# FFT mixing and a three-way maxout network on one core: how the first batch's rows are fetched, cast and reversed

## Chip, core and metric

One core of one Trainium2 chip runs the whole program. The metric is the device time of one execution in microseconds (us). The core has five engines with queues of their own: TensorE (PE, matmuls; its weight loads are listed as PEld), VectorE (DVE), ScalarE (ACT), GpSimd (POOL) and SyncE (SP). DMA transfers are issued here by SP, ACT and POOL, and are carried out by 16 DMA engines that all queues share. Each engine works through its own instructions in order; engines wait for each other through semaphores.

## What is computed

```python
def _attn_ref(x):                       # x: 8 x 3072 x 256, fp32
    X = np.fft.fft(x, axis=1)
    X = np.fft.fft(X, axis=2)
    return X.real.astype(np.float32)

def _moe_ref(x, w1, w2, w3, w_out):     # 24576 tokens, 256 -> 768 -> 256
    h = np.maximum(np.maximum(x @ w1, x @ w2), x @ w3)
    return (h @ w_out).astype(np.float32)
```

The output is `_moe_ref` of the tokens that `_attn_ref` gives.

## The kernel before

A batch of x is 3072 rows of 256 features. The row number is split as 128 a + bb (a below 24, bb below 128), the feature number as 64 g + dl (g below 4). A batch lies in SBUF on 96 partitions (g, a), and each partition holds 128 pieces ("rows" bb) of 64 features dl. The Fourier transform over the row number is done in two steps, first over a (24 values, `Mix.s`), then over bb (128 values, `Mix.k`); the transform over the features is folded into the network's weights (`prep_first`, `prep_second`). Because x is real, the kernel works on x and on x with its rows in reverse order: `Mix.s` multiplies, for each dl, the forward rows (line 415) and the reversed rows of the mirrored feature 64 - dl (line 417), and accumulates both. For batches 1 to 7 POOL makes the bf16 copies of x, forward and reversed, while PE works on the batch before (`turn_chunk`).

Batch 0 has nothing to hide behind, and is handled apart, in the straight code that the change touches:

- Rows 0 to 79 are loaded by POOL (lines 178, 186, 190), which casts them to bf16 on the way, straight into the forward tile `x0_first` (`x0`, `x0v`). `load_rows` issues four transfers, one for each g, of 24 partitions each.
- Rows 80 to 127 are loaded as fp32 into the staging tiles `xs` by SP and ACT (lines 163 to 170), and row 128, which is row 0 of the next a, by `load_next`: four transfers of 23 partitions and one of 4. Here rows 80 to 95 go by SP, 96 to 111 by ACT, then by SP row 128 and after it rows 112 to 127.
- The reversed rows lie in `back` (`xr0`), one line of 130 rows for each dl from 32 to 64. `reverse(copy, xr, xs, r0, n, d0, d1)` writes the reversed copy of rows r0 to r0 + n - 1 for dl from d0 to d1 - 1; the engine is the one whose `copy` it is given.
- The staged rows are cast into `x0_first` by DVE (line 331) and reversed for dl 32 to 63 by ACT (line 332). Then ACT makes `md_all`, the sines of the feature angles (line 333), and the rest is reversed from `x0_first` by ACT and DVE (lines 334 to 339).
- The feature angles `vm` (lines 309 to 326) are made on DVE, ahead of the casts. `nmd_all` is `md_all` negated (line 340), `tab_minus` negates a part of the sine table of the second step (lines 307, 341).
- While rows arrive, PE runs 17 matmuls on the sine table whose result is not used (`warm`, lines 608 to 610). Then come the groups s0 to s6 of batch 0 (line 614; s0 uses dl 2 to 6, and so reversed dl 58 to 62; s1 uses dl 7 to 11), the first folded weights (line 617) and the steps of the second transform.
- SP, after the transfers of batch 0, loads batch 1 (line 348), each of these transfers behind the landing of the weights' first half. POOL, after the rows, issues the weights (lines 193 to 201).

The order on each engine is the order of the program's text; nothing is rescheduled.

Of the kernel before, what the change touches and what calls it, by code (L numbers as in the profile page):

```python
# [9 lines left out]
FP32 = mybir.dt.float32  # L10
BF16 = mybir.dt.bfloat16
# [22 lines left out]
def kernel(  # L34
# [9 lines left out]
    nc = tc.nc  # L44
# [48 lines left out]
    def x_rows(b):  # L93
        return x[b].rearrange("(a bb) (g dl) -> g a bb dl", bb=128, g=4)

    def load_rows(eng, dst, b, r0, r1, after=None):
        xr = x_rows(b)
        for g in range(4):
            ld = eng.dma_start(out=dst[g * 24:(g + 1) * 24], in_=xr[g, :, r0:r1, :])  # L99
            if after is not None:  # L100
                tc.add_manual_dep(ld.ins, after.ins.name, AFTER, reason="weights first")

    def load_next(eng, dst, b, after=None):

        xr = x_rows(b)
        parts = [(dst[g * 24: g * 24 + 23], xr[g, 1:24, 0:1, :]) for g in range(4)]
        parts.append((dst[23:96:24], xr[:, 0, 0:1, :]))
        for (to, src) in parts:
            ld = eng.dma_start(out=to, in_=src)
            if after is not None:  # L110
                tc.add_manual_dep(ld.ins, after.ins.name, AFTER, reason="weights first")
# [13 lines left out]
    def reverse(copy, xr, xs, r0, n, d0=32, d1=65):  # L125

        last = r0 + n > 128
        for (lo, hi, m) in ((d0, min(d1, 64), n), (64, d1, n - 1)) if last else ((d0, d1, n),):
            if lo < hi:
                copy(out=xr[:, lo - 32:hi - 32, 129 - r0 - m:129 - r0],  # L130
                     in_=bass.AP(xs.tensor, xs.offset + (m - 1) * 64 + lo,
                                 [xs.ap[0], [1, hi - lo], [-64, m]]))
# [19 lines left out]
    gen = gen_pool_cm.__enter__()  # L152
# [3 lines left out]
    def iota(t, pattern, base=0, cm=0):  # L156
        nc.gpsimd.iota(t, pattern, base=base, channel_multiplier=cm,
                       allow_small_or_imprecise_dtypes=True)

    x0_first = x0_pool.tile([96, 64 * 130], BF16, name="x0", tag="x0")  # L160
    x0v = x0_first.rearrange("p (bb dl) -> p bb dl", dl=64)
    staged = []
    for (r0, eng) in ((80, nc.sync), (96, nc.scalar), (112, nc.sync)):
        n = 17 if r0 == 112 else 16
        xs = xs_pool.tile([96, 33 * 64], FP32, name="xs", tag="xs")
        xv = xs[:, 0:n * 64].rearrange("p (bb dl) -> p bb dl", dl=64)
        if n > 16:
            load_next(eng, xv[:, 16:17, :], 0)
        load_rows(eng, xv[:, 0:16, :], 0, r0, r0 + 16)
        staged.append((r0, n, xs))  # L170

    pidx = gen.tile([128, 1], FP32, tag="pidx")
    iota(pidx, [[0, 1]], cm=1)
# [1 line left out]
    iota(j128, [[1, 128]])  # L175
    i13 = gen.tile([128, 13], FP32, tag="i13")
    iota(i13, [[1, 13]])
    load_rows(nc.gpsimd, x0v[:, 0:32, :], 0, 0, 32)
    jm24 = gen.tile([96, 48], FP32, tag="jm24")
    iota(jm24[:, 0:13], [[1, 13]])  # L180
    iota(jm24[:, 13:24], [[-1, 11]], base=-1)
# [1 line left out]
    iota(jm24[:, 37:48], [[1, 11]], base=1)  # L183
    g24 = gen.tile([96, 5], FP32, tag="g24")
    iota(g24, [[24, 5]])
    load_rows(nc.gpsimd, x0v[:, 32:64, :], 0, 32, 64)
    dvec = gen.tile([128, 128], FP32, tag="dvec")
    iota(dvec.rearrange("p (dl g) -> p dl g", g=4), [[1, 32], [64, 4]])
    iota(dvec[:, 2:4], [[64, 2]], base=32)
    load_rows(nc.gpsimd, x0v[:, 64:80, :], 0, 64, 80)  # L190

    first_half = None
    for jh in range(2):
        for wsrc, wdst in ((moe_w1, w1_bf), (moe_w2, w2_bf), (moe_w3, w3_bf)):
            wld = nc.gpsimd.dma_start(
                out=wdst.rearrange("p (fc j) -> p fc j", fc=2)[:, :, jh * 384:(jh + 1) * 384],
                in_=wsrc.rearrange("(fc p) j -> p fc j", fc=2)[:, :, jh * 384:(jh + 1) * 384])
        if jh == 0:
            first_half = wld
    nc.gpsimd.dma_start(out=wout_bf.rearrange("p (jc c) -> p jc c", jc=NJC),  # L200
                        in_=moe_w_out.rearrange("(jc p) c -> p jc c", jc=NJC))
# [16 lines left out]
    nc.vector.memset(z[:, :, 24:26], 0.0)  # L218
    nc.vector.memset(m0f[:, 50:52], 0.0)
    nc.vector.memset(m0r[:, 50:52], 0.0)  # L220
    half = gen.tile([128, 256], FP32, tag="half")
    nc.vector.memset(half[:, 0:128], 64.0)
    nc.vector.memset(half[:, 128:256], 0.0)

    p128 = gen.tile([128, 1], FP32, tag="p128")
    nc.vector.tensor_scalar(out=p128, in0=pidx, scalar1=1.0 / 128.0, scalar2=None, op0=ALU.mult)
# [30 lines left out]
    def tab_minus(r0, r1):  # L257
        nc.vector.tensor_scalar(out=tabs[:, r0:r1, 2, :], in0=tabs[:, r0:r1, 0, :],
                                scalar1=-1.0, scalar2=None, op0=ALU.mult)
# [36 lines left out]
    for (m, c, by) in ((m24f, 0, ind24), (m24r, 24, ind24[:, ::-1])):  # L296
        nc.vector.tensor_tensor(
            out=m.rearrange("p (g r) -> p g r", g=4),
# [7 lines left out]

    tab_minus(0, 7)

    vm = gen.tile([128, 512], FP32, tag="vm")
    qm = gen.tile([128, 512], FP32, tag="qm")  # L310
    pf = gen.tile([128, 2], FP32, tag="pf")
    half = gen.tile([128, 256], FP32, tag="half")
    nc.vector.memset(half[:, 0:128], 64.0)
    nc.vector.memset(half[:, 128:256], 0.0)
    for fc in range(2):
# [3 lines left out]
            out=vm[:, fc * 256:(fc + 1) * 256].rearrange("p (k c) -> p k c", c=128),  # L319
# [5 lines left out]
    nc.vector.scalar_tensor_tensor(out=vm, in0=qm, scalar=-256.0 * ROUND, in1=vm,  # L325
                                   op0=ALU.add, op1=ALU.subtract)

    back = gen.tile([96, 33 * 130], BF16, tag="back")
    xr0 = back.rearrange("p (dl bb) -> p dl bb", bb=130)
    for (r0, n, xs) in staged:  # L330
        nc.vector.tensor_copy(out=x0_first[:, r0 * 64:(r0 + n) * 64], in_=xs[:, 0:n * 64])
        reverse(nc.scalar.copy, xr0, xs, r0, n, 32, 64)
    nc.scalar.activation(out=md_all, in_=vm, func=AX.Sin, scale=float(-2.0 * math.pi / 256.0))
    for (copy, r0, n, d0, d1) in ((nc.scalar.copy, 80, 49, 64, 65),
                                  (nc.scalar.copy, 0, 31, 32, 65),
                                  (nc.vector.tensor_copy, 31, 32, 32, 65),
                                  (nc.scalar.copy, 63, 17, 32, 49),
                                  (nc.vector.tensor_copy, 63, 17, 49, 65)):
        reverse(copy, xr0, x0_first[:, r0 * 64:(r0 + n) * 64], r0, n, d0, d1)
    nc.vector.tensor_scalar(out=nmd_all, in0=md_all, scalar1=-1.0, scalar2=None, op0=ALU.mult)  # L340
    tab_minus(7, 13)
    nc.vector.tensor_scalar(out=sgn, in0=pidx, scalar1=0.0, scalar2=None, op0=ALU.is_equal)
# [263 lines left out]
                l2_queue.pop(0)  # L606

    warm = ps_s.tile([128, 512], FP32, name="warm", tag="ps")
    for _ in range(17):
        nc.tensor.matmul(warm, tab[:, 0:128], tab[:, 0:512], start=True, stop=True)  # L610
    m = Mix(0)
    x0f = (lambda d: x0v[:, 0:128, d], rows_back(xr0))
# [150 lines left out]
```

## Time and profile before

| | |
|---|---|
| runs | 429.35, 429.67, 430.62 us; median 429.67 us |
| the profiled execution | 428.75 us, of which the profile's span is 427.0 us |
| PE busy | 407.5 us (95%), 3073 matmuls |
| DVE, ACT, POOL busy | 274.1 us (64%), 258.1 us (60%), 244.3 us (57%) |
| the chain that ended last, by engine | PE 94%, POOL 2%, DMA 2%, ACT 1% |
| PE busy from 0 to 20 us | 6.16 us, 5.90 of them in the warm matmuls |
| PE busy from 60 to 420 us | 359.76 of 360 us |

The span is the time from the first to the last instruction of the program; the execution's own time is 1.75 us longer. In the lines of the profile, "L415" is line 415 of the kernel, "x17" a number of instructions, "out<-in" the tiles written and read with partitions x elements and type, and what stands in brackets is the idle time of the engine just before and what ended it. "SPq" and "ACTq" are issues of transfers; the time beside them is that of issuing, not of the transfer. PE's clock is given as a share of its full rate.

### The profile page before, as it was taken

What the parts mean: (1) busy time and instruction counts of PE and PEld (TensorE: products, weight loads), DVE (VectorE), ACT (ScalarE), POOL (GpSimd) and SP (SyncE); (2) the same over time, 40 slices, a digit from 0 to 9 for tenths busy, and PEclk for the clock granted to TensorE, in tenths of its full rate; (3) what the DMA queues carried; (4) which work ended last, traced back from release to release, by engine and by line L of the source; (5) the groups of instructions that cost most, each with busy time, mean ns of one, the idle gap of its engine ahead of it and who ended that gap; (6) DMA issues with size and microseconds to landing.
All of it is one profiled execution on the core that took longest, in us unless ns stands there. A gap on an engine that the chain in (4) does not pass through costs nothing.

```text
span 427.0 us, 8732 instructions
## 1 busy us (share of the span) xinstructions
PE 407.5 (95%) x3073; PEld 271.5 (64%) x3073; DVE 274.1 (64%) x455; ACT 258.1 (60%) x477; POOL 244.3 (57%) x291
## 2 busy tenths in 40 slices
PE   0699999999999999999999999999999999999996
PEld 0275667666676666666666666666666666666665
DVE  8747566565666665676656665675656665666773
ACT  6736666666666666656665566647665666655550
POOL 9639655973279625983289624983289622214320
PEclk9989999999999999999999999999999999999999
DMA  9998893594217941498217851387311221212223
GB/s 131 130 170 176 169 230 111 141 217 103 98 72 169 202 134 52 109 206 168 99 61 169 207 141 51 96 199 179 107 55 71 64 74 63 74 51 58 93 74 124
DMA packets 130180, 52.28 MB, mean 122 GB/s; under 512 B 112081, under 2 KB 127192, under 8 KB 130136
## 3 DMA queue, kind: packets, MB, share of 16 engines
q1 hardware_dynamic: 107784, 36.52, 36.6%
q0 software_dynamic: 20624, 14.68, 15.0%
q10 hardware_dynamic: 1728, 0.52, 0.6%
q8 instruction: 24, 0.39, 0.4%
q14 instruction: 20, 0.16, 0.1%
HBM read 29.02 MB, written 25.17 MB: 127 GB/s over the span
## 4 chain that ended last, share of the span: by engine, by line
PE 94%; POOL 2%; DMA 2%; ACT 1%; DVE 0%; issue 0%; POOLq 0%
PE po L485 29%; PE pse L461 15%; PE pse L462 15%; PE pse L469 14%; PE po L509 5%; PE ps L415 3%; PE ps L417 3%; PE ps L443 3%; PE ps L441 2%; PE pl L501 2%; POOL x L99 2%; DMA x<-in_x_dram 2%; PE psg L361 1%; ACT back L130 0%; PE pst L380 0%
## 5 line engine op out<-in xcount | busy, mean ns | idle before, releaser
L475 ACT ACTIVATE stmp<-pse 128x512 bf16<-128x512 f32 x288 | 171.5, 600 | 52.7 <-PE pse L462 47.0
L519 POOL DMA_INDIRECT out_dram<-ot,rows_m x92 | 100.4, 1091 | 160.7 <-DVE ot L514 145.0
L476 DVE TENSOR_TENSOR hp<-pse,stmp 128x512 bf16<-128x512 f32 x144 | 99.5, 691 | 129.8 <-ACT stmp L475 91.4
L461 PE MATMUL pse<-t,gE 128*128 128x512 bf16 x288 | 109.2, 379 | 1.0 <-ACT gO L368 0.6
L462 PE MATMUL pse<-t,gO 128*128 128x512 bf16 x288 | 109.0, 378 | 0.0
L476 DVE TENSOR_TENSOR hm<-pse,stmp 128x512 bf16<-128x512 f32 x144 | 99.2, 689 | 6.8 <-ACT stmp L475 6.7
L485 PE MATMUL po<-wout_bf,hp 128*128 128x256 bf16 x576 | 86.1, 273 | 0.0
L469 PE MATMUL pse<-t,gD 128*128 128x512 bf16 x288 | 85.6, 379 | 0.0
L485 PE MATMUL po<-wout_bf,hm 128*128 128x256 bf16 x576 | 78.6, 273 | 0.0
L485 PEld LDWEIGHTS <-hp 128*128 128x128 bf16 x576 | 56.4, 98 | 26.1
L485 PEld LDWEIGHTS <-hm 128*128 128x128 bf16 x576 | 56.4, 98 | 16.3
L514 DVE TENSOR_TENSOR ot<-po,even 128x512 f32<-128x512 f32 x92 | 62.8, 683 | 0.0
L145 POOL CAST x<-xs 96x1056 bf16<-96x1056 f32 (+1 forms) x35 | 58.3, 1677 | 0.0
L143 POOL CAST x<-xs 96x1056 bf16<-96x1056 f32 x28 | 56.7, 2027 | 0.0
L445 ACT CAST t<-ps 128x512 bf16<-128x512 f32 x47 | 27.5, 586 | 43.3 <-PE ps L443 43.1
L422 ACT CAST z_all<-ps 128x480 bf16<-128x480 f32 x45 | 25.2, 559 | 43.1 <-PE ps L417 43.1
L469 PEld LDWEIGHTS <-gD 128*128 128x128 bf16 x288 | 27.9, 98 | 32.2
L462 PEld LDWEIGHTS <-gO 128*128 128x128 bf16 x288 | 28.1, 98 | 20.4 <-issue 2.0
L461 PEld LDWEIGHTS <-gE 128*128 128x128 bf16 x288 | 28.1, 98 | 19.5 <-issue 0.4
L509 PE MATMUL po<-gw,t 128*128 128x512 bf16 x92 | 34.9, 379 | 0.0
L415 PE MATMUL ps<-m24f,x 96*128 96x96 bf16 (+1 forms) x256 | 29.8, 213 | 2.0 <-DMA w_bf<-in_moe_w_dram 2.0
L415 PEld LDWEIGHTS <-x 96*128 96x128 bf16 x264 | 25.3, 106 | 3.0 <-DVE back L130 2.5
(137 smaller groups left out, 325.4 us busy)
## 6 DMA issues: line engine op xcount, KB each, us to landing
xs<-in_x_dram SPq DMA_DIRECT2D x84, 198.0 KB
out_dram<-ot SPq DMA_DIRECT2D x90, 128.0 KB
xs<-in_x_dram SPq DMA_DIRECT2D x28, 192.0 KB
out_dram<-ot,rows_m POOLq DMA_INDIRECT x92, 2.9
w_bf<-in_moe_w_dram POOLq DMA_DIRECT2D x6, 192.0 KB, 5.7
out_dram<-ot SPq DMA_DIRECT2D x17, 64.0 KB
xs<-in_x_dram SPq DMA_DIRECT2D x8, 96.0 KB
x<-in_x_dram POOLq DMA_DIRECT2D x8, 96.0 KB, 7.9
```

The source lines that it names most:

```text
L143: nc.gpsimd.tensor_copy(v[:, 0:33, ch * 32:ch * 32 + 32], xs[:, 0:32 * 64].rearrange("p (bb dl) -> p dl bb", dl=64)[:, 0:33, :])
L145: reverse(lambda out, in_: nc.gpsimd.tensor_copy(out, in_), v[:, 33:66, :], xs, ch * 32, 33 if ch == 3 else 32)
L415: nc.tensor.matmul(ps1[:, c0:c0 + n], x0[0](d), mf[:, 0:n], start=True, stop=False)
L461: nc.tensor.matmul(pse[:, 0:n], gE[i][:, js], te, start=True, stop=False)
L462: nc.tensor.matmul(pse[:, 0:n], gO[i][:, js], to, start=False, stop=True)
L469: nc.tensor.matmul(pse, gD[i][:, js], to, start=False, stop=True, skip_group_check=True)
L475: nc.scalar.activation(out=stmp[:, 0:n], in_=pses[0][:, 0:n], func=AX.Relu)
L476: nc.vector.tensor_tensor(out=dst, in0=src3, in1=stmp[:, 0:n], op=ALU.max)
L485: nc.tensor.matmul(po, hcols(jc), wout_bf[:, jc * 256:(jc + 1) * 256], start=False, stop=(jc == NJC - 1), skip_group_check=True)
L509: nc.tensor.matmul(po, to[:, cp], gw[:, 256:768], start=True, stop=True)
L514: nc.vector.tensor_tensor(out=ot.rearrange("p (h c) -> p h c", h=2), in0=po.rearrange("p (h c) -> p h c", h=2), in1=lin.unsqueeze(1).to_br ...
L519: stored(nc.gpsimd.indirect_dma_start(out, bass.IndirectOffsetOnAxis(ap=rows_m[0:128 - lo, b * 12 + slot: b * 12 + slot + 1], axis=0), ot[ ...
```

## The change

Four things are altered, all in the start of the program.

- **Transfers.** SP loads rows 80 to 111 in four transfers and ACT rows 112 to 127 in four; row 128 follows on SP, behind the rows. POOL loads rows 0 to 47 and 48 to 79 in four transfers each, the second four behind all its iotas. Without row 128, that is 16 transfers in place of 24.
- **Engines.** The staged rows are cast by ACT and reversed by DVE for dl 32 to 63. Of the rows that POOL loaded, ACT reverses dl 54 to 64 and DVE dl 32 to 53; dl 64 of rows 80 to 128 goes to DVE.
- **Order.** Casts and reversals of the staged rows stand ahead of the feature angles `vm` on DVE; the reversals of rows 0 to 46 stand behind the angles on DVE, and ahead of `md_all` on ACT; rows 47 to 79 come last.
- **Small things.** A second, unused setting of `half` goes (two memsets), and there are 19 warm matmuls in place of 17.

```diff
-    for (r0, eng) in ((80, nc.sync), (96, nc.scalar), (112, nc.sync)):
-        n = 17 if r0 == 112 else 16
+    for (r0, r1, eng) in ((80, 112, nc.sync), (112, 128, nc.scalar)):
+        n = r1 - r0
         xs = xs_pool.tile([96, 33 * 64], FP32, name="xs", tag="xs")
-        xv = xs[:, 0:n * 64].rearrange("p (bb dl) -> p bb dl", dl=64)
-        if n > 16:
-            load_next(eng, xv[:, 16:17, :], 0)
-        load_rows(eng, xv[:, 0:16, :], 0, r0, r0 + 16)
+        load_rows(eng, xs[:, 0:n * 64].rearrange("p (bb dl) -> p bb dl", dl=64), 0, r0, r1)
         staged.append((r0, n, xs))
+    load_next(nc.sync, xs[:, n * 64:(n + 1) * 64].rearrange("p (n d) -> p n d", n=1), 0)
+    staged[-1] = (r0, n + 1, xs)
...
-    load_rows(nc.gpsimd, x0v[:, 0:32, :], 0, 0, 32)
+    load_rows(nc.gpsimd, x0v[:, 0:48, :], 0, 0, 48)
...
-    load_rows(nc.gpsimd, x0v[:, 32:64, :], 0, 32, 64)
...
-    load_rows(nc.gpsimd, x0v[:, 64:80, :], 0, 64, 80)
+    load_rows(nc.gpsimd, x0v[:, 48:80, :], 0, 48, 80)
...
-    half = gen.tile([128, 256], FP32, tag="half")
-    nc.vector.memset(half[:, 0:128], 64.0)
-    nc.vector.memset(half[:, 128:256], 0.0)
...
     tab_minus(0, 7)
 
+    back = gen.tile([96, 33 * 130], BF16, tag="back")
+    xr0 = back.rearrange("p (dl bb) -> p dl bb", bb=130)
+
+    def turn_rows(copy, r0, n, d0, d1):
+        reverse(copy, xr0, x0_first[:, r0 * 64:(r0 + n) * 64], r0, n, d0, d1)
+
+    for (r0, n, xs) in staged:
+        nc.scalar.copy(out=x0_first[:, r0 * 64:(r0 + n) * 64], in_=xs[:, 0:n * 64])
+        reverse(nc.vector.tensor_copy, xr0, xs, r0, n, 32, 64)
+
     vm = gen.tile([128, 512], FP32, tag="vm")
...
-    back = gen.tile([96, 33 * 130], BF16, tag="back")
-    xr0 = back.rearrange("p (dl bb) -> p dl bb", bb=130)
-    for (r0, n, xs) in staged:
-        nc.vector.tensor_copy(out=x0_first[:, r0 * 64:(r0 + n) * 64], in_=xs[:, 0:n * 64])
-        reverse(nc.scalar.copy, xr0, xs, r0, n, 32, 64)
+    turn_rows(nc.scalar.copy, 0, 47, 54, 65)
+    turn_rows(nc.vector.tensor_copy, 80, 49, 64, 65)
+    turn_rows(nc.vector.tensor_copy, 0, 47, 32, 54)
     nc.scalar.activation(out=md_all, in_=vm, func=AX.Sin, scale=float(-2.0 * math.pi / 256.0))
-    for (copy, r0, n, d0, d1) in ((nc.scalar.copy, 80, 49, 64, 65),
-                                  (nc.scalar.copy, 0, 31, 32, 65),
-                                  (nc.vector.tensor_copy, 31, 32, 32, 65),
-                                  (nc.scalar.copy, 63, 17, 32, 49),
-                                  (nc.vector.tensor_copy, 63, 17, 49, 65)):
-        reverse(copy, xr0, x0_first[:, r0 * 64:(r0 + n) * 64], r0, n, d0, d1)
+    turn_rows(nc.scalar.copy, 47, 33, 54, 65)
+    turn_rows(nc.vector.tensor_copy, 47, 33, 32, 54)
...
-    for _ in range(17):
+    for _ in range(19):
         nc.tensor.matmul(warm, tab[:, 0:128], tab[:, 0:512], start=True, stop=True)
```

## The prediction

> **What bounds the kernel now.** I read the stage table first (windows of the span), then the chain of waits in order of time, then the timeline of the first 21 us, then the trace's packet records by queue.
>
> ```profile
> 0.00:10.00 10.00, 0.00 (x0) 0.00 (x0) 8.78 (x32) 6.14 (x7) 8.98 (x23) 1.00 1.26 130
> 10.00:20.00 10.00, 6.16 (x18) 2.27 (x18) 7.69 (x22) 7.15 (x14) 6.15 (x9) 1.00 1.44 132
> 20.00:30.00 10.00, 8.79 (x90) 7.37 (x91) 4.35 (x10) 4.74 (x10) 4.13 (x9) 0.83 1.14 169
> 30.00:40.00 10.00, 10.00 (x58) 5.79 (x58) 6.74 (x11) 6.48 (x12) 8.35 (x6) 1.00 0.83 168
> ```
>
> Columns: stretch, length, busy PE, PEld, DVE, ACT, POOL, granted clock, DMA share, GB/s. From 30 us PE is busy all the time (10.00 of 10.00; 359.76 of 360 from 60 to 420 us). So whatever moves the first real matmul moves the end by the same amount, and only the first 20 us, where the DMA engines are full (share above 1), can change the time.
>
> ```profile
> 12.04 6.55 DMA x<-in_x_dram
> 18.58 2.02 ACT back L130 x2
> 20.65 0.22 PE ps L417
> ...
> 11.71 5.90 PE L610 MATMUL warm<-tab 128*128 128x512 bf16 x17 [11.71 <-DVE tab L258]
> 13.91 0.69 DVE L325 SCALAR_TENSOR_TENSOR vm<-qm,vm 128x512 f32<-128x512 f32 x1
> 16.88 1.18 ACT L130 CAST back<-xs 96x544 bf16<-96x544 f32 x1 [2.82 <-DMA xs<-in_x_dram]
> 17.96 0.63 ACT L333 ACTIVATE md_all<-vm 128x512 bf16<-128x512 f32 x1
> 18.49 2.69 ACT L130 COPY back<-x 96x48 bf16<-96x48 bf16 x3
> 19.31 0.40 DVE L130 COPY back<-x 96x272 bf16<-96x272 bf16 x1 [0.24 <-DMA x<-in_x_dram]
> ```
>
> The mix starts at 20.65, the first reversed matmul (L417). Its chain: the last fp32 rows land at 16.88; ACT, in order, reverses them (1.18), makes md_all (0.63), then copies 48 and 1023 elements (0.26 and 1.94) until 20.59. The rows that POOL loads are a second limit, close by: the last land at 19.0 and 19.19, after which DVE needs 0.40. The angles vm are no limit: DVE makes them from 11.54 to 14.61, while it waits for rows.
>
> **Why those rows land at 16.88.** The packet records tell it. Each transfer of 24 partitions posts 12 completions (48 four-byte packets for the four transfers of ACT's queue): it runs on 12 DMA engines. Each 23-partition piece of load_next posts one: its 23 packets run on a single engine, one after the other (8.61 to 9.47: 39 ns apiece beside POOL's packets). SP's queue holds, for that engine, 128 packets (rows 80 to 95, through at 6.6), then 93 (load_next, 8.05 to 10.4), then 128 (rows 112 to 127, last at 16.3). POOL's packets run from 5 us on and never run dry: 6144 are issued by 8.83, some 2700 started.
>
> ```profile
> 0.74 1.81 SPq L99 DMA_DIRECT2D xs<-in_x_dram  x4
> 3.76 3.04 SPq L109 DMA_DIRECT2D xs<-in_x_dram  x5
> 6.85 36.87 SPq L99 DMA_DIRECT2D xs<-in_x_dram  x20
> 1.49 3.57 POOL L99 DMA_DIRECT2D x<-in_x_dram  x4 [0.21 <-issue]
> 5.57 3.26 POOL L99 DMA_DIRECT2D x<-in_x_dram  x4
> 9.55 1.38 POOL L99 DMA_DIRECT2D x<-in_x_dram  x2
> ```
>
> **The change, part by part.**
>
> *Transfers.* The bytes and packets are the same: 4608 row packets from SP and ACT, 7680 from POOL, 93 on the one engine. POOL's issue shortens. A 32-row transfer takes 0.82 and a 16-row one 0.68, so a 48-row one is some 0.96 (first 1.20): 1.49 + 4.08, iotas 0.5 and 0.72, four of 0.82: done at 10.1, not 12.71. Nothing is gained by it, because the queue is backed up anyway; the busiest engine carries 384 + 93 + 480 = 957 packets in either order and ended at 18.66. So I keep the last landing of POOL's rows at 19.2 (bounds 17.7 to 19.8: the median engine's 17.3 to 17.5 plus little, or 0.6 later if issue order costs what the straggler lost).
>
> *load_next goes behind the rows.* SP's queue on the one engine is now 256 row packets, then 93. By 6.6 it has done 128, as now. The other 128 go at 36 to 39 ns (rows 112 to 127 now: 32 per engine in some 1.15 us): 4.6 to 5.0, and 0.6 more because ACT's queue shares the engine until some 8.4: 11.8 to 12.2. Then 93 x 39 ns = 3.6: 15.4 to 15.8. Landing is 0.45 later (9.51 to 9.96 now). Row 128 of x thus lands at 15.9 to 16.3; I take **16.1**. Bounds: 14.6 if its packets go at 14.5 ns apiece for half the way, as the first 23 did (8.05 to 8.37), and 18.0 if they go at 1.1 us per 23 (landings 8.80, 9.96, 11.04) behind a row queue that is a microsecond slower.
>
> *DVE now waits for it ahead of the angles.* The reversals of both staged tiles stand ahead of vm. Behind the waiting instruction on DVE are the whole vm chain, three reversed copies, nmd_all, tab_minus(7, 13); on ACT, md_all waits for vm, and behind md_all stands the copy of rows 47 to 79 for dl 54 to 64, which the first mix matmul (dl 58 to 62) needs. From row 128's landing: semaphore 0.05; reversal of 544 fp32 elements on DVE, which the trace does not show. From DVE's reversed bf16 copies (1056 in 1128 ns, 272 in 395: 141 ns + 0.935 an element) 0.65; bounds 0.36 (the contiguous cast, 1088 in 723 ns) and 1.18 (ACT's own). Less 0.05 of overlap. Then vm, 11.54 to 14.61 less the 0.12 it waited for dvec: 2.94. Then 0.05; md_all to the next start 0.53 (17.96 to 18.49); 363 elements on ACT: from 1023 in 1942 and 289 in 682 ns, 1.72 an element + 0.19: 0.81; 0.06 to PE. Sum **5.04**; PE starts at 16.1 + 5.04 = 21.14, **0.49 later** than 20.65.
>
> *ACT's casts.* 2048 elements 2.03 and 1088 1.13 (from 896 in 0.95 and 768 in 0.83). The first runs from some 12.6 and the second ends at 17.2; then the copy of rows 0 to 46 (517 elements, 1.07) until 18.3. All hidden behind vm, which is ready at 19.7. Without that cover ACT would start the last copy when the last rows land: 19.2 + 0.05 + 0.81 + 0.06 = 20.1, a floor 0.55 ahead of now.
>
> *Off the path.* DVE's 1034 and 726 elements (1.11, 0.82) end at 21.7 and are first needed by the second group, 1.35 x 2 after PE starts; two memsets of 0.17 go, and DVE waits for iotas there; two more warm matmuls at 0.216 end at 18.04 on an idle PE. Weights follow POOL's rows in one queue and are first used at 25.4. Each of these: 0.
>
> *Clock.* PE's clock was 0.5 for one stretch of 3.41 us (22.76 to 26.17 in the clock records). It cost about 0.8: matmul pairs at 0.16 for 0.135 us, and three L361 at 0.32 for 0.16. I take it as unchanged; bounds -0.8 (it goes away) and +1.7 (one more on full-rate work).
> The Trainium skill (TensorE: Matmul & The Clock Gate, Part 1) says that the clock drops after an idle window of about 3.4 us. In this trace a pause of 3.04 us, with one matmul in it, preceded the half rate; by that rule the pause of 3.1 forecast here gives one such window again, the sum above.
>
> Sum: +0.49. The profiled execution took 428.75 (span 427.0 and 1.75 around it): 429.24. It lies 0.92 under the median of the runs, 429.67; against that the forecast is **430.2**.
>
> **Rivals.** *Row 128 early* (chance 0.22): it lands by 15.0, since SP's queue no longer stands empty from 6.6 to 8.05. Then POOL's last rows decide, PE starts at 20.1, 429.1. Against it: 1.4 us saved there are needed by ACT's queue, which is served meanwhile. *Row 128 late* (0.23), the slower side: three queues share its engine until the ACT rows are through, row 128 lands at 18.0, the angles wait with it: 18.0 + 5.04 = 23.04, +2.4, 432.1. It decides from a landing at 16.9 on (PE at 21.94, +1.29). For it: each later piece of load_next took 1.1 us beside POOL's packets. Against it: rows 112 to 127 kept a steadier pace. *Fewer transfers bring x sooner* (0.10): the engines gain from longer runs, the rows land 1.5 us earlier on both paths; PE starts at 18.6 to 19.6 and the half-rate stretch shrinks: -1.0 to -2.0 and -0.8, about 427.3. Against it: the engines are full from 2 to 18 us, and per-packet times do not depend on the transfer's size.
> The Trainium skill (DMA: Bandwidth & Descriptors, Rules for kernel authors) tells to coalesce small transfers, since under 64 KB they are mostly overhead; by it this rival would be the forecast. Four of the 24 transfers are below that size (48 KB), and they landed within 1.1 us of each other.
>
> **How the numbers follow.** Forecast 0.45, rivals 0.22, 0.23, 0.10. About 0.3% (1.3 us, 428.4 to 431.0) is what a measurement of this kernel tells from no change. Faster: 0.10 and a little of the first rival, 0.13. Slower: 0.22 of the second and the upper end of the forecast's bounds (clock, reversal), 0.30. Within: 0.57. The range goes from 428.4 to 432.2: it takes in both neighbours' times and leaves out the third rival and a second clock drop. The forecast's own range is 429.4 to 431.0.
>
> **What would show it.** In the changed kernel: DVE idle ahead of its second reversal from xs, ended by a transfer of xs at 15.9 to 16.3; vm (L325's line) ending 3.6 us after; md_all right behind it on ACT; the first L417 near 21.1, released by ACT's copy. POOL's x issues done near 10.1 and its last x landing still near 19. Wrong: if that idle time ends before 15, if L417 waits for a transfer of x, or if DVE's reversal of 544 fp32 elements is over 1 us; and the sum would be wrong throughout if PE shows new idle time after 30 us.

## The result: 0.3% slower, and where the time went

Over 20 executions each, the changed kernel took 431.57 us in the median (429.69 to 434.53) and the kernel before 430.56 (429.08 to 431.38): ratio 1.0030, 95% interval 1.0015 to 1.0044. A second set, on one chip, gave 430.57 (12 executions) against 429.35 (35): 1.0031 (1.0020 to 1.0042). So some 1.0 to 1.3 us were added; the forecast was +0.5. The profiled execution took 431.12 us with a span of 429.4.

The stage table of the changed kernel (stretch, length, busy PE, PEld, DVE, ACT, POOL, granted clock, DMA share, GB/s):

```profile
0.00:10.00 10.00, 0.00 (x0) 0.00 (x0) 8.32 (x31) 6.59 (x7) 9.06 (x22) 1.00 1.09 135
10.00:20.00 10.00, 6.05 (x19) 2.19 (x19) 4.71 (x15) 5.70 (x11) 3.84 (x7) 1.00 2.01 125
20.00:30.00 10.00, 8.32 (x83) 7.25 (x84) 6.10 (x13) 4.10 (x9) 4.17 (x8) 0.66 1.08 167
30.00:40.00 10.00, 9.43 (x55) 5.21 (x53) 6.10 (x10) 5.67 (x11) 7.43 (x5) 1.00 0.80 168
...
60.00:420.00 360.00, 359.48 (x2736) 239.66 (x2735) 231.24 (x358) 222.75 (x417) 202.91 (x235) 1.00 0.44 116
```

DVE was busy for 4.71 us of the second ten microseconds, in place of 7.69: it stood and waited. PE's clock in the third was 0.66 in place of 0.83. From 60 us on PE is full, as before.

The chain of waits of the changed kernel (start, length, what):

```profile
10.06 6.57 DMA xs<-in_x_dram
16.85 0.64 DVE back L130
17.89 0.49 DVE vm L323
18.66 0.50 DVE vm L323
19.37 0.44 DVE qm L329
19.83 0.70 DVE vm L330
20.67 0.41 issue
21.09 0.81 ACT back L130
21.95 0.26 PE ps L416
```

The timeline of DVE and ACT in the same kernel (start, length, engine, line, operation, out<-in; in brackets the idle time before):

```profile
12.41 1.08 DVE L130 CAST back<-xs 96x1024 bf16<-96x1024 f32 x1 [1.30 <-DMA xs<-in_x_dram]
16.85 0.64 DVE L130 CAST back<-xs 96x544 bf16<-96x544 f32 x1 [3.35 <-DMA xs<-in_x_dram]
17.46 0.17 DVE L318 MEMSET half<- 128x128 f32 x1
...
19.83 0.69 DVE L330 SCALAR_TENSOR_TENSOR vm<-qm,vm 128x512 f32<-128x512 f32 x1
...
16.81 1.10 ACT L311 CAST x<-xs 96x1088 bf16<-96x1088 f32 x1 [2.52 <-DMA xs<-in_x_dram]
18.14 1.08 ACT L130 COPY back<-x 96x517 bf16<-96x517 bf16 x1 [0.24 <-DMA x<-in_x_dram]
20.55 0.63 ACT L336 ACTIVATE md_all<-vm 128x512 bf16<-128x512 f32 x1 [1.33 <-DVE vm L330]
21.09 0.81 ACT L130 COPY back<-x 96x363 bf16<-96x363 bf16 x1
```

The two views tell the same story. The last piece of row 128 is issued at 10.06 and lands at 16.63. DVE idles 3.35 us for it, reverses, and only then makes the angles; ACT idles 1.33 us for the angles before md_all, and the copy behind md_all lets PE start at 21.95, 1.30 later than before.

In this pair of profiles the first network matmul (tile pse) starts at 32.00 in place of 29.96 (2.04 later). 1.30 of it is PE's start, the other 0.74 the clock: half rate for 6.83 us here, for 3.41 us in the profile of before. The last matmul ends 2.62 later. The missing 0.58 arise at about 148 us and belong to this one execution: from the first pse matmul to its last PE needs 394.1 us here, and 393.5 to 393.6 in the profile of before and in a second profile of the changed kernel.

### The profile page after: what moved, and what is told of

The parts are those of the page before. It is cut to its first block, busy times and chain, and to the rows that moved or that the text cites. A ratio compares the mean times of both kernels' runs of the same rounds, so it can differ in the third digit from the quotient of the medians.

```text
span 429.4 us, 8713 instructions
## 1 busy us (share of the span) xinstructions
PE 408.7 (95%) x3075; PEld 271.8 (63%) x3075; DVE 273.8 (64%) x453; ACT 257.0 (60%) x475; POOL 243.1 (57%) x287
## 4 chain that ended last, share of the span: by engine, by line
PE 93%; DMA 3%; DVE 1%; SPq 1%; ACT 1%; issue 0%; DVEq 0%; ACTq 0%
PE po L484 29%; PE pse L460 15%; PE pse L468 14%; PE pse L461 14%; PE po L508 5%; PE ps L416 3%; PE ps L414 3%; DMA xs<-in_x_dram 3%; PE pl L500 3%; PE ps L442 2%; PE ps L440 2%; PE psg L360 1%; SPq L109 1%; DVE hm L475 0%; PE pst L379 0%
```

## The experiments

Theory: the angles, put behind the staged reversals on DVE, wait for row 128, whose small transfers are last in SP's queue. Rivals: POOL's last rows set the start (they landed at 20.27, a microsecond later than before); or the loss is PE's clock. All ratios are to the kernel before, on the chip of the run.

| run | median us | ratio (95%) | row 128 lands | first reversed matmul | from it to first pse | half rate before 60 us |
|---|---|---|---|---|---|---|
| before (profile) | | | 11.56 | 20.65 | 9.31 | 3.41 |
| changed | 431.57 | 1.0030 (1.0015 to 1.0044) | 16.63 | 21.95 | 10.05 | 6.83 |
| changed, again | 430.57 | 1.0031 (1.0020 to 1.0042) | 17.14 | 22.46 | 9.03 | 3.41 |
| angles first | 429.26 | 0.9992 (0.9977 to 1.0008) | 17.58 | 21.11 | 10.36 | 6.83 |
| row 128 cut finer | 433.14 | 1.0085 (1.0069 to 1.0100) | 19.59 | 24.76 | 9.97 | 10.24 |
| both | 431.45 | 1.0056 (1.0042 to 1.0069) | 19.29 | 22.68 | 9.48 | 6.83 |
| row 128 at the head | 430.72 | 1.0034 (1.0021 to 1.0048) | 5.94 | 22.74 | 10.22 | 6.83 |
| 33 warm matmuls | 429.40 | 1.0012 (0.9995 to 1.0030) | 17.24 | 22.57 | 8.51 | 0 |
| before + POOL's transfers | 430.25 | 1.0018 (1.0005 to 1.0030) | 11.74 | 20.70 | 10.82 | 6.83 |
| before + SP's and ACT's transfers | 428.01 | 0.9977 (0.9963 to 0.9992) | 15.83 | 20.32 | 9.12 | 3.41 |
| the same, 27 warm | 428.42 | 0.9958 (0.9945 to 0.9971) | 15.95 | 20.60 | 8.55 | 0 |
| angles first, 33 warm | 428.63 | 0.9968 (0.9956 to 0.9980) | 16.07 | 20.73 | 8.51 | 0 |
| and md_all early | 428.62 | 0.9965 (0.9953 to 0.9978) | 15.83 | 21.09 | 8.52 | 0 |
| before, 27 warm | 429.72 | 0.9988 (0.9976 to 1.0001) | 11.93 | 20.82 | 10.79 | 6.83 |

The four columns on the right are of one profiled execution each. In the kernel before, and in the two runs that leave SP's queue as it was, rows 112 to 127 come after row 128 (16.86 in the profile of before).

### Angles first

```diff
-    for (r0, n, xs) in staged:
-        nc.scalar.copy(...)
-        reverse(nc.vector.tensor_copy, xr0, xs, r0, n, 32, 64)
-
     vm = gen.tile([128, 512], FP32, tag="vm")
...
+    for (r0, n, xs) in staged:
+        nc.scalar.copy(...)
+        reverse(nc.vector.tensor_copy, xr0, xs, r0, n, 32, 64)
+
     turn_rows(nc.scalar.copy, 0, 47, 54, 65)
```

> The changed kernel with one thing moved: on DVE the feature angles stand ahead of the two reversals of the staged rows. Theory (the angles wait behind row 128): DVE idles for the rows as long as now, but nothing stands behind that wait; the angles are ready by 15 us, md_all no longer sets the last copy on ACT, and the first reversed matmul follows the last landing of POOL's rows (20.27 in the changed kernel) by 0.05 + 0.81 + 0.06: 21.2, in place of 21.95; time 0.75 us below the changed kernel, about 430.8, still not below the kernel before. Rival (DVE's reversals themselves, or ACT's casts, set the start): the first reversed matmul stays at 21.9 to 22.0 and the time at 431.6.

The timeline of DVE and ACT in this run:

```profile
13.46 0.69 DVE L326 SCALAR_TENSOR_TENSOR vm<-qm,vm 128x512 f32<-128x512 f32 x1
...
17.80 0.63 DVE L130 CAST back<-xs 96x544 bf16<-96x544 f32 x1 [2.66 <-DMA xs<-in_x_dram]
...
17.76 1.10 ACT L330 CAST x<-xs 96x1088 bf16<-96x1088 f32 x1 [2.47 <-DMA xs<-in_x_dram]
18.76 1.07 ACT L130 COPY back<-x 96x517 bf16<-96x517 bf16 x1
19.73 0.64 ACT L336 ACTIVATE md_all<-vm 128x512 bf16<-128x512 f32 x1
20.26 0.80 ACT L130 COPY back<-x 96x363 bf16<-96x363 bf16 x1
```

Row 128 was later than in the changed kernel's profile (DVE starts on it at 17.80 in place of 16.85), and still PE starts 0.84 earlier. The clean reading is the distance from DVE's second reversal to PE's start: 5.10 us in both profiles of the changed kernel (16.85 to 21.95, and 17.36 to 22.46 in the one shown further down), 3.31 here. So the order alone costs 1.79 us of start. The ratio agrees: 0.9992 against 1.0030, 0.4% or 1.6 us, which brings the kernel back to the time of before, twice what was expected for that one landing. The theory stands, with one correction to the expectation: what is left is not POOL's rows but ACT's queue behind row 128, which has no idle time in these lines (cast, copy, md_all, copy: 3.3 us).

### Row 128 cut finer

```diff
+    def load_next_spread(eng, dst, b):
+        xr = x_rows(b)
+        for g in range(4):
+            for (a0, a1) in ((0, 12), (12, 23)):
+                eng.dma_start(out=dst[g * 24 + a0: g * 24 + a1],
+                              in_=xr[g, 1 + a0:1 + a1, 0:1, :])
+        eng.dma_start(out=dst[23:96:24], in_=xr[:, 0, 0:1, :])
...
-    load_next(nc.sync, xs[:, n * 64:(n + 1) * 64].rearrange("p (n d) -> p n d", n=1), 0)
+    load_next_spread(nc.sync, xs[:, n * 64:(n + 1) * 64].rearrange("p (n d) -> p n d", n=1), 0)
```

> The changed kernel with load_next's 23-partition transfers of batch 0 each cut into 12 and 11 partitions. Theory (93 packets one after the other on a single DMA engine): row 128 lands at 12.5 to 13.5 in place of 16.63, DVE's second reversal starts by 14, vm is done by 17.5; and the engine that was last with POOL's rows has 85 packets less, so that their last landing comes from 20.27 to 18.7 to 19.3 and the first reversed matmul to 19.7 to 20.3: 1.7 to 2.2 us less than the changed kernel, 429.4 to 429.9. Rival (the rows of SP are late for lack of bandwidth, whichever engine carries them): row 128 lands after 15.5, the start is at 21 or later, the gain under 0.9 us.

This missed, by far: the ratio rose from 1.0030 to 1.0085, by 0.55% or some 2.4 us. SP's timeline of this run:

```profile
0.73 3.71 SPq L99 DMA_DIRECT2D xs<-in_x_dram  x4
5.08 8.65 SPq L117 DMA_DIRECT2D xs<-in_x_dram  x8
14.10 0.73 SPq L119 DMA_DIRECT2D xs<-in_x_dram  x1
```

and DVE's:

```profile
19.62 0.62 DVE L138 CAST back<-xs 96x544 bf16<-96x544 f32 x1 [4.99 <-DMA xs<-in_x_dram]
```

SP's and ACT's transfers share eight semaphores here, and a transfer is issued only when the previous one with its semaphore has landed. With nine pieces in place of five, the eighth waited for a row transfer (landed 13.43) and the ninth for the first piece (14.08). Issued at 13.45 and 14.10, into a system full of POOL's packets, these two landed at 18.6 and 19.59: 5 us for 11 and 4 packets. The single engine alone was thus not what held row 128: even the first seven pieces, which post 12 or 11 completions each, landed at 14.1 to 16.7, when 12.5 to 13.5 was expected. What held is the other half of the expectation's reading: POOL's last rows came earlier (19.0 in place of 20.27), and the distance from DVE's reversal to PE's start was 5.14 us (19.62 to 24.76), as without the cut.

### Both edits

> Both edits: angles ahead of the staged reversals, and load_next cut into 12 and 11 partitions. Theory (with row 128 early, the order on DVE has nothing left to cost): the same as the cut alone, within 0.3 us, 429.4 to 429.9. Rival (the two costs add): 0.7 us below the cut alone.

The two edits above together gave 1.0056, 0.29% under the cut alone: the rival's side, but not for the rival's reason. Row 128 was not early (19.29), so the order still had its cost to give back: 3.36 us from DVE's reversal (19.32) to PE's start, as with the angles first alone.

### Row 128 at the head of SP's queue

```diff
-    for (r0, r1, eng) in ((80, 112, nc.sync), (112, 128, nc.scalar)):
+    staged_xs = [xs_pool.tile([96, 33 * 64], FP32, name="xs", tag="xs") for _ in range(2)]
+    load_next(nc.sync, staged_xs[1][:, 16 * 64:17 * 64].rearrange("p (n d) -> p n d", n=1), 0)
+    for (r0, r1, eng, xs) in ((80, 112, nc.sync, staged_xs[0]), (112, 128, nc.scalar, staged_xs[1])):
         n = r1 - r0
-        xs = xs_pool.tile([96, 33 * 64], FP32, name="xs", tag="xs")
...
-    load_next(nc.sync, xs[:, n * 64:(n + 1) * 64].rearrange("p (n d) -> p n d", n=1), 0)
```

> The changed kernel with the transfers of row 128 at the head of SP's queue instead of its end. Theory (what costs is that row 128 comes after 3072 packets in SP's queue, and its small transfers are issued late into a full one): row 128 lands by 5 us, rows 80 to 111 by 13 to 14.5, DVE has reversed both by 16 and has the angles by 18.5; the start is then set by POOL's last rows (20.3) and comes at 21.0 to 21.3; time 0.7 to 1.5 us below the changed kernel of the same chip. Rival (the 93 packets on one engine delay the rows behind them by as much as they are earlier): rows 80 to 111 land after 16, no gain.

The rival's times held, but not its reason. DVE's timeline of this run:

```profile
16.55 1.63 DVE L130 CAST back<-xs 96x1024 bf16<-96x1024 f32 x2 [4.66 <-DMA xs<-in_x_dram]
```

Row 128 is there at 5.94, but rows 80 to 111 now land at 16.35 (12.29 in the changed kernel), and the angles wait behind them instead. The delay went from one transfer to another; the time is that of the changed kernel (1.0034). What the trace shows of the cause is the eight semaphores again: SP's third transfer of rows was issued at 4.65, when the third piece of row 128 had landed (4.64) and freed its semaphore, and the fourth at 6.26; in the changed kernel they were issued at 1.75 and 2.75. That the 93 packets on one engine held the rows back is not shown.

### The changed kernel again

> The changed kernel unaltered, beside the kernel before and the three below on one chip. Theory (its start depends on when row 128 lands, which differs between executions: 16.6 in the profile of the changed kernel, 17.4 and 17.6 in two experiments that left its transfers alone): ratio to the kernel before between 1.002 and 1.006; in its profile the first reversed matmul comes 5.0 to 5.2 us after the last landing of load_next, wherever that is. Rival (a fixed delay): the first reversed matmul at 21.9 to 22.0 again, with load_next landing elsewhere.

DVE's second reversal in this run:

```profile
17.36 0.63 DVE L130 CAST back<-xs 96x544 bf16<-96x544 f32 x1 [3.23 <-DMA xs<-in_x_dram]
```

The first reversed matmul came at 22.46, 5.10 after DVE's reversal and 5.32 after row 128's landing at 17.14 (5.32 in the first profile, too: 16.63 to 21.95); the expectation's 5.0 to 5.2 was 0.1 to 0.3 short. The fixed delay is refuted. Row 128's landing varies: 15.83 to 17.58 over the profiles that have the changed kernel's transfers unaltered.

### POOL's transfers alone, SP's and ACT's alone

Both are the kernel before with one part of the new loads (the lines of the diff above), and its own order on DVE and ACT.

> The kernel before with POOL's transfers of the change alone (rows 0 to 47 and 48 to 79 in four each). POOL is done issuing near 10. Theory A (the fp32 rows in SP's queue hold POOL's rows back in the changed kernel): POOL's last landing stays at 19.0 to 19.4 and the time within 0.3 us of the kernel before. Theory B (a 48-row transfer starts later and makes the last landing late): last landing at 19.8 or later, time 0.4 to 0.9 us above it.

> The kernel before with SP's and ACT's transfers of the change alone (rows 80 to 111 on SP, 112 to 127 on ACT, row 128 behind). DVE still makes the angles first and casts, ACT still reverses. Theory A: POOL's last landing comes at 19.8 to 20.4. Theory B: 19.0 to 19.4. In both, row 128 lands at 16.5 to 17.5, ACT reverses the second tile at once, then md_all and two copies: first reversed matmul 3.8 us after that landing, 20.4 to 21.3, time -0.2 to +0.7 us against the kernel before: the late row costs little where no angles stand behind it.

SP's and ACT's part alone is a gain: 0.9977 (0.9963 to 0.9992). ACT's timeline of that run:

```profile
16.00 1.18 ACT L130 CAST back<-xs 96x544 bf16<-96x544 f32 x1 [1.67 <-DMA xs<-in_x_dram]
17.08 0.62 ACT L332 ACTIVATE md_all<-vm 128x512 bf16<-128x512 f32 x1
17.61 2.74 ACT L130 COPY back<-x 96x48 bf16<-96x48 bf16 x3
```

The last staged row is in at 15.83, one microsecond before the 16.86 of the kernel before, and ACT's chain starts 0.88 earlier. POOL's last landing was 19.25, as theory B had it for this run. Three things missed: row 128 was earlier than the 16.5 to 17.5 expected, the gain larger (1.0 us, where -0.2 to +0.7 was expected), and the first reversed matmul came 4.5 us after the landing in place of 3.8. ACT's copy of rows 0 to 30, which set PE's start in the kernel before (until 20.59), ends at 19.78 here. The start, 20.32, now follows DVE's copy of POOL's last rows:

```profile
19.78 0.39 DVE L130 COPY back<-x 96x272 bf16<-96x272 bf16 x1 [0.74 <-DMA x<-in_x_dram]
```

So PE starts only 0.33 earlier, and the first pse matmul comes 0.52 earlier, than in the profile of before; these two executions do not show the rest of the 1.0 us.

POOL's part alone cost 0.18% (0.05 to 0.30). Its last landing was early, 18.74, which fits neither theory. The run doesn't price the transfers cleanly: the old reversal of rows 31 to 62 on DVE now needs the second group of transfers, so that it started at 18.97, a microsecond late, and PE's start (20.70) is that of the kernel before. The half-rate stretch was the longer one.

### The clock

The changed kernel with 33 warm matmuls in place of 19:

> The changed kernel with 33 warm matmuls in place of 19. Theory (part of the loss is PE's clock: 6.83 us at half rate after the pause, against 3.41 us in the kernel before): the warm matmuls end near 20, PE starts at 21.95 as now, no stretch at half rate before 60 us, and the time is 1.0 to 1.6 us below the changed kernel, 430.0 to 430.6. Rival (the first groups are bound by weight loads, the clock costs next to nothing): half rate gone, time within 0.3 us of the changed kernel.

```diff
-    for _ in range(19):
+    for _ in range(33):
```

The stage table of this run, and of angles first:

```profile
20.00:30.00 10.00, 9.14 (x96) 7.34 (x95) 6.99 (x16) 4.43 (x9) 4.66 (x7) 1.00 1.12 162
```

```profile
20.00:30.00 10.00, 9.15 (x86) 7.60 (x87) 4.63 (x12) 4.13 (x9) 3.98 (x9) 0.66 0.98 150
```

The clock is the number after the five engines: 1.00 here, 0.66 there. From the first reversed matmul to the first pse matmul PE needs 8.51 us at full rate, and 9.0 to 10.8 with a half-rate stretch (table). The time falls by 0.18% against the changed kernel's ratio (1.0012 against 1.0030), 0.8 us, a little less than expected; the two intervals overlap, so the ratios alone do not prove it.

The single executions say more. Half rate ahead of 60 us shows in the mean granted clock of an execution: the profiles without it have 0.998 to 1.000, those with 3.41 us 0.994 to 0.996, those with 6.83 us 0.990 to 0.992. Of the 35 executions of the kernel before on one chip, 15 have 0.994 to 0.996 and take 428.69 us in the mean, 20 have 0.990 to 0.992 and take 429.73. So a further 3.41 us at half rate goes with 1.0 us of time, and the kernel before pays, too:

> The kernel before with 27 warm matmuls in place of 17. Theory (the clock's cost is no part of the change, since the kernel before pays one half-rate stretch of 3.4 us, in some executions two): half rate gone, first pse matmul 8.5 us after the first reversed one in place of 9.3, ratio 0.997 to 0.9985. Rival (the kernel before loses nothing there): 0.9995 to 1.0005.

With 27 warm matmuls the kernel before came to 0.9988 (0.9976 to 1.0001), inconclusive; its own profile shows 6.83 us at half rate although PE paused for only 1.2 us (19.60 to 20.82, one matmul between). That profile does not stand for all: by the mean granted clock, half rate is gone in 5 of the 12 executions (0.999 and 1.000).

### Versions that beat both

> The kernel before with SP's and ACT's transfers of the change (the faster of the runs so far, ratio 0.9977) and 27 warm matmuls in place of 17. Theory (the half-rate stretch after the pause costs 0.5 to 1.5 us a time in every one of these kernels): warm ends at 18.5 to 20.1, the first reversed matmul at 20.3 as without it, no half rate before 60 us, the first pse matmul 8.5 us after it in place of 9.1: 0.4 to 1.0 us less than without the extra matmuls, ratio to the kernel before 0.995 to 0.997, below both kernels. Rival (the clock's share is small or the pause still halves it): ratio 0.997 to 0.999.

> The changed kernel with the angles ahead of the staged reversals and 33 warm matmuls. Theory (the wait of the angles and the clock are two costs, one on the start and one after it): they add. Angles first gave 0.4% against the changed kernel, the warm matmuls 0.2%: ratio 0.997 to 0.998. Rival (with an earlier start the pause is short enough anyway): as angles first alone, 0.999. The warm matmuls may end at 21.5, after the rows are ready (21.1), which would cost up to 0.4.

> As the run with angles first and 33 warm matmuls, and md_all ahead of ACT's cast of the second staged tile, where ACT waits for row 128 anyway. Theory (with the angles early, ACT's queue behind row 128 sets the start: cast 1.1, copy 1.07, md_all 0.53, copy 0.8): one 0.53 less, the first reversed matmul at 20.6 to 20.9 (last landing of POOL's rows 19.9, and 0.86), held up to 21.5 only by the warm matmuls; time 0 to 0.4 below the run without it. Rival (POOL's last rows set the start): no difference.

The kernel before with SP's and ACT's new transfers and 27 warm matmuls is the fastest run of the study: 428.42 us against 430.27 on its chip, 0.9958 (0.9945 to 0.9971). Angles first with 33 warm matmuls adds its two gains, as expected, to 0.9968. With md_all moved ahead of the second cast there was no further gain (0.9965), but that run can't tell: ACT's last copy was done early,

```profile
19.02 0.82 ACT L130 COPY back<-x 96x363 bf16<-96x363 bf16 x1 [0.93 <-DMA x<-in_x_dram]
```

and PE started only at 21.09, when the warm matmuls ended. The bracket shows the next limit: with md_all out of the way, ACT waits 0.93 us for POOL's last rows. Fewer warm matmuls in this version were not tried.

## Why the prediction was right, and what it mis-sized

The path was forecast, and the size fell short: +0.5 us against the measured +1.0 to +1.3. The time still lies in the range (428.4 to 432.2); the first set's 431.57 lies above the forecast's own 429.4 to 431.0, in the part that the range kept for a late row 128.

- **The mechanism and its price.** It was forecast that the angles wait on DVE behind row 128, and that md_all and the last copy follow, 5.04 us from landing to PE's start. Measured 5.32 from the landing, 5.10 of it from the start of the reversal on. The terms: reversal 0.65, measured 0.64; angles 2.94, measured 3.06 (17.46 to 20.52; the 0.12 that was to fall away, the pause before L323, stayed); md_all and copy 0.53 and 0.81, measured 0.54 and 0.81. The rest is 0.2 between the last completion and DVE's start, where 0.05 was set.
- **Row 128's landing**, forecast 16.1, was 16.63 and 17.14 in the two profiles of the changed kernel, 15.83 to 17.58 over all that share its transfers. This is the term that was mis-sized, and most of the difference between +0.49 and +1.30 at PE's start. The sum took load_next's 93 packets as back to back behind the rows. They were not quite: the trace has a gap of 0.51 us between the third and fourth piece's packets, and the fourth piece landed at 16.23 (16.56 in the second profile). The last transfer, of 4 partitions, came later still: it posts four completions, at 15.49, 15.58, 15.72 and 16.63, the last 0.40 behind the fourth piece (0.58 in the second profile), where the sum counted its packets as the last four of the 93, 0.16 us. SP was held up while issuing (5.87 us for the five, the fourth piece until 10.02); whether the gap comes from that is not shown. The queue's pace itself, 39 ns a packet, was right.
- **POOL's last rows**, forecast 19.2 (17.7 to 19.8), landed at 20.27 and, in the second profile, 19.70. POOL was done issuing at 10.19 (10.1 forecast), and that gained nothing, as argued. The landing at 20.27 would have held PE to 21.2, so that the forecast's floor of 20.1 was too low.
- **The clock**, taken as unchanged, added 0.74 in the first profile and none in the second (3.41 us at half rate there), although PE's pause was 4.65 us in both, not the 3.1 forecast. Against the same kernel with few warm matmuls, the ratio fell by 0.12 to 0.24% in the four versions tried, the kernel before among them, so most of the clock's price is no part of the change. A small part may be: on the second set's chip, 10 of the changed kernel's 12 executions have a mean granted clock of 0.990 to 0.992, against 20 of 35 before. Among these alone the changed kernel is 0.9 us slower (means of 430.66 and 429.73), over all executions 1.3 (430.58 and 429.28), which leaves an estimate of 0.4 us for the clock.
- **The rivals.** Of the three, row 128 late came closest. The forecast let it decide from a landing at 16.9 on, with PE at 21.94; the two profiles lie on either side of that landing (16.63 and 17.14, PE at 21.95 and 22.46), and the measured +1.0 to +1.3 lies between the forecast's +0.5 and the rival's +2.4. Row 128 early did not happen, and fewer transfers brought x no sooner as a whole: SP's and ACT's part is a gain of 0.23%, POOL's part alone a loss.
The Trainium skill (DMA: Bandwidth & Descriptors, Rules for kernel authors) would have small transfers joined; here the run with fewer and larger transfers on SP and ACT was faster and the one with fewer on POOL was not (both change more than the sizes), and nine small transfers in place of five cost 0.55%.
- **What the change would be worth in parts.** SP's and ACT's transfers gained some 1.0 us, the place of the angles cost 1.6; POOL's transfers and the exchange of ACT and DVE make up the remaining 0.7 or so, which no clean run divides. These are differences of ratios with intervals of 0.1 to 0.2%, so each figure is an estimate.

## What to carry to other kernels

Before moving a waiting instruction ahead of ready work on an in-order engine, count all that stands behind it: here 3 us of angles, which had been free because they filled the wait, moved onto the path. The distance from the wait's end to the first matmul was constant (5.10 to 5.14 in four profiles) while the landing moved by microseconds, so an order is best judged by that distance, and not by one execution's total. Cutting a small transfer that everything waits for did not bring it sooner: each piece needed a free semaphore, and the last two took over 5 us beside a full queue. Its place in the queue mattered less than what waits for it: at the head of SP's queue it made the rows behind it late, and in the fastest version it is still last, but no angles stand behind it.

## What was not expected of the hardware

A transfer of 4 packets, issued at 14.10 while POOL's queue was full, landed 5.5 us later, and one of 11 partitions, issued at 13.45, 5.2 us later.

The half-rate stretches lasted 3.41, 6.83 or 10.24 us, and each began 6.83 us after full rate had been granted (14.90 and 21.73 in the changed kernel, 15.93 and 22.76 in the kernel before), whether PE's pause in between had been 1.2 us or 7.8. With pauses of 1.4 us (fastest run) and 1.2 us (kernel before, 27 warm), one matmul in each, one profile has no half rate and the other 6.83 us of it. What decides between these two stayed open.

The Trainium skill (TensorE: Matmul & The Clock Gate, Part 1) lets the clock drop after an idle window of about 3.4 us; the profile with the pause of 1.2 us shows it dropping after about a third of that, and the measurement decides.
